# The second layer's first product in seven half-size products per pair of token tiles (Strassen) instead of eight

## The chip, the cores and the metric

The kernel runs on one core of one Trainium2 chip. The metric is the device time of one execution in microseconds, lower is better. Before the change three runs took 957.3, 959.89 and 960.03 us; their median, 959.89 us, is the time before.

## The reference

Three layers run one after the other, all in float32.

```
attn: state = gamma[h]*state + k_t v_t^T ;  y_t = scale * q_t state      (B,H,S,D = 4,8,768,64)
x  = y as (3072, 512)
ff1: x = elu(x @ w_in) @ w_out                                           (512 -> 2048 -> 512)
ff2: h = x @ w_in2                                                       (512 -> 1024)
     e = exp(h - max h);  solu = h * e / (sum e + 1e-9)
     ln = (solu - mean) / sqrt(var + 1e-6) * g_ln ;  out = ln @ w_out2   (1024 -> 512)
```

The weights arrive as float64; the kernel turns them into float32 itself.

## The kernel before

Every float32 operand of the two feed-forward layers is split into a high part of type fp32r and a low part, the rest. A product is then three matmuls (`mm3`, L63 to L67): high by high, high by low, low by high.

**FF1** works on six blocks (`tb`) of 512 tokens with 16 steps each, one step `s` per 128 hidden columns: `ff1_in(s)` (L255) is 12 matmuls into one of two PSUM banks `hp`, `elu_a` and `elu_b` (L265, L274) compute the activation on ScalarE and VectorE, GpSimd subtracts the high part to get `gl` (L290), and two steps later `ff1_out(s-2)` (L296) adds 12 matmuls into four banks `acc`. A bank `hp` is free for `ff1_in(s+2)` when `elu_b(s)` has read it. After a block, y goes to DRAM. Attention for later tokens runs between the steps of the first five blocks.

**FF2** works on 24 tiles of 128 tokens (L521 to L540). For tile `i`, `load_y` and `split_y` fetch and split y; `ff2_in(i)` (L333) makes h (128 tokens by 1024) in 24 matmuls; `norm_a` and `norm_b` (L342, L359) are max, exp, the product z, its mean and the sum of squares; `transpose(i-1)` (L367) transposes the z of the tile before in 8 matmuls, ScalarE and VectorE split it (`zh`, `zl`), and `ff2_out(i-2)` (L379) is 24 matmuls. The banks of h alternate between two places (`psr` and `ps2`).

**Weights.** `prep_w(order, n)` (L128) is a pipeline by slots: in slot `n`, ScalarE takes the absolute value of weight `n+1` and GpSimd clamps it (`clamp_w`, L98), VectorE builds the float32 bits of weight `n` in three instructions (`bits_w`, L104 to L108), the high part of weight `n-2` is a ScalarE copy and the low part a VectorE subtraction (L117, L125), and SyncE issues the load of weight `n+3`. The 16 weights of FF2 (`order2`: 8 of `w2i`, then 8 of `w2o`, which are first multiplied by `g_ln`, L114) are prepared during FF1's last block, one slot per step.

Nothing is reordered by a scheduler: each engine executes its instructions in the order in which the code writes them, and waits on semaphores between engines.

Of the kernel before, what the change touches and what calls it, by code (L numbers as in the profile page):

```python
# [43 lines left out]
def tile_retention_ffn(ctx, tc, k_t, qk_dup, qkv, w_in1, w_out1, w_in2, w_out2, g_ln, dmask, odec, kdec, ident_in, out):  # L44
# [5 lines left out]
    wa_p = ctx.enter_context(tc.tile_pool(name="wa", bufs=32))  # L50

# [17 lines left out]
    with tc.manual_schedule():  # L69
        ph1 = ExitStack()  # L70
        psh = ph1.enter_context(tc.tile_pool(name="psh", bufs=2, space=PSUM))
        ps = ph1.enter_context(tc.tile_pool(name="ps1", bufs=1, space=PSUM))
        pha = ExitStack()
# [3 lines left out]
        wb_p = ph1.enter_context(tc.tile_pool(name="wb", bufs=32))  # L77
        x_p = ph1.enter_context(tc.tile_pool(name="x", bufs=1))
# [10 lines left out]
        raw_t, abs_t, w1i, w1o, w2i, w2o = {}, {}, {}, {}, {}, {}  # L89
        srcs = {"w1i": w_in1, "w1o": w_out1, "w2i": w_in2, "w2o": w_out2}  # L90
        dsts = {"w1i": w1i, "w1o": w1o, "w2i": w2i, "w2o": w2o}
# [6 lines left out]
        def clamp_w(x):  # L98
            a = stage_p.tile([P, 512], U32, tag="wt", name="wt")
            nc.scalar.activation(a.bitcast(F32), raw_t[x][:, :, 1].bitcast(F32), AF.Abs)  # L100
            nc.gpsimd.tensor_scalar(a.bitcast(F32), a.bitcast(F32), E_MAX, E_MIN, ALU.min, ALU.max)
            abs_t[x] = a

        def bits_w(x):  # L104
            t, b = raw_t.pop(x), abs_t[x]
            nc.vector.tensor_scalar(b, b, 3, 0x3FFFFFF8, ALU.logical_shift_left, ALU.bitwise_and)
            nc.vector.scalar_tensor_tensor(b, t[:, :, 1], 0xC0000000, b, ALU.bitwise_and, ALU.bitwise_or)  # L107
            nc.vector.scalar_tensor_tensor(b, t[:, :, 0], 29, b, ALU.logical_shift_right, ALU.bitwise_or)  # L108

        def high_w(x):  # L110
            name, f = x
            w = abs_t[x].bitcast(F32)
            if name == "w2o":
                nc.vector.tensor_scalar(w, w, g_sb[:, f:f + 1], None, ALU.mult)  # L114
            pool, tag = (wb_p, "wb") if name == "w1o" else (wa_p, "wa")
            hi = pool.tile([P, 512], F32R, tag=tag, name=f"{name}h")
            nc.scalar.copy(hi, w)  # L117
            dsts[name][f] = hi

        def low_w(x):  # L120
            name, f = x
            w, hi = abs_t.pop(x).bitcast(F32), dsts[name][f]
            pool, tag = (wb_p, "wb") if name == "w1o" else (wa_p, "wa")
            lo = pool.tile([P, 512], F32R, tag=tag, name=f"{name}l")
            nc.vector.tensor_tensor(lo, w, hi.bitcast(F32), ALU.subtract)  # L125
            dsts[name][f] = (hi, lo)

        def prep_w(order, n):  # L128

            at = lambda i: order[i] if 0 <= i < len(order) else None  # L130
            if at(n - 2):
                high_w(at(n - 2))
# [4 lines left out]
            if at(n - 2):  # L137
                low_w(at(n - 2))
            if at(n + 3):
                load_w(at(n + 3))  # L140
# [4 lines left out]
        order2 = [("w2i", j) for j in range(2 * KD)] + [("w2o", j) for j in range(NF2)]  # L145
# [150 lines left out]
        def ff1_out(s):  # L296
# [8 lines left out]
            if f == NF1 - 1:  # L305
                for m in range(KD):
                    yt = yt_p.tile([P, TB], F32, tag="yt", name="yt", bufs=3) if m < 3 else e_p.tile([P, TB], F32, tag="e", name="yt")
# [12 lines left out]
        def load_y(i):  # L320
            t = yi_p.tile([P, KD, P], F32, tag="yin", name="yin")
            nc.sync.dma_start(out=t, in_=y_dr[i // CPB][i % CPB])
            yin[i] = t

        def split_y(i):
            t = yin.pop(i)
            yh = ys_p.tile([P, KD, P], F32R, tag="yh", name="yh")
            yl = ys_p.tile([P, KD, P], F32R, tag="yl", name="yl")
            nc.vector.tensor_copy(yh, t)
            nc.gpsimd.tensor_tensor(yl, t, yh.bitcast(F32), ALU.subtract)  # L330
            ysp[i] = (yh, yl)

        def ff2_in(i):  # L333
            yh, yl = ysp.pop(i)
            hp = (psr if i % 2 == 0 else ps2).tile([P, 2, 512], F32, tag="hp", name="hp2", bufs=1)
            for n in range(2):
                for cc in range(KD):
                    wh, wl = w2i[2 * cc + n]
                    mm3(hp[:, n, :], yh[:, cc, :], yl[:, cc, :], wh, wl, cc == 0, cc == KD - 1)
            h2[i] = hp  # L340

        def norm_a(i):  # L342
            hp = h2.pop(i)
            st = sm_p.tile([P, 8], F32, tag="st", name="st")
            if i == 0:
                e, z = xf[:, :2], xf[:, 2:]
# [32 lines left out]
        def ff2_out(i, kks=range(NF2)):  # L379
            zh, zl = zt_t[i]  # L380
# [56 lines left out]
        for s in range(NS + LAG):  # L437
            tb, k = divmod(s, NF1)
            n = PPB + LEAD + s
            u = n // 2  # L440
            if s < NS:
                ff1_in(s)
                elu_a(s, tb == 0)
                if k == NF1 - 1 and tb + 1 < NB:
                    split_xh(tb + 1, range(KD))
                    elu_b(s, tb == 0)
# [17 lines left out]
            if s < NS and (k < NF1 - 1 or tb + 1 == NB):  # L464
                elu_b(s, tb == 0)
            if s == NS + LAG - 1:
                ff2_in(0)
                split_y(2)
                norm_a(0)
                norm_b(0)  # L470
# [24 lines left out]
            if n == NPR - 1:  # L495
# [13 lines left out]
                prep_w(order2, -1)  # L509
            if tb == NB - 1:  # L510
                prep_w(order2, k)
                if k in (1, 2, 3):
                    load_y(k - 1)
                if k in (9, 11):
                    split_y((k - 9) // 2)
            if tb == NB:
                prep_w(order2, NF1 + k)
# [3 lines left out]
        for i in range(N2):  # L521
            if i + 3 < N2:
                load_y(i + 3)
            if i == 0:
                continue
            ff2_in(i)
            if i == 1:
                norm_a(i)
            if i + 2 < N2:
                split_y(i + 2)  # L530
            transpose(i - 1)
            if i > 1:
# [69 lines left out]
```

## Time and profile before

| | |
|---|---|
| runs, us | 957.3, 959.89, 960.03 (median 959.89) |
| the profiled execution | 957.76 us, of which the span of instructions is 955.9 us |
| TensorE busy | 928.9 us, 97% of the span, 4776 matmuls |
| VectorE, ScalarE, GpSimd busy | 494.7, 347.4 and 341.5 us |
| FF1's last block | about 573 to 663 us of the span |
| FF2 | from about 668 us to the end |

Matmuls are pipelined, so the recorded length of one overlaps the next; what one costs is the distance between two starts. A line of the timeline is one instruction, with its start, its length, engine, line, operands, and in brackets the idle time ahead of it. On VectorE and GpSimd a recorded length includes the time in which an instruction that was already issued waited inside the engine.

### The profile page before, as it was taken

The numbers are of one execution on the slowest core, as the hardware profiler recorded it, in microseconds if no ns is written. First come the engines' busy times: TensorE is split into PE (matmuls) and PEld (weight loads), VectorE is DVE, ScalarE is ACT, GpSimd is POOL, SyncE is SP. The second block draws the span as 40 slices with busy tenths as digits, with TensorE's granted clock in tenths as the row PEclk, the third lists the DMA queues.
The fourth block names the chain that finished last, engine by engine and source line by source line (L and its number), as shares of the span: only waits on it lengthen the run. The fifth ranks groups of instructions, "written<-read, shape, count | busy, mean of one in ns | idle before, by whom it ended". The sixth has DMA issues, their size and how long they took to land.

```text
span 955.9 us, 12630 instructions
## 1 busy us (share of the span) xinstructions
PE 928.9 (97%) x4776; PEld 760.0 (80%) x4776; DVE 494.7 (52%) x973; ACT 347.4 (36%) x629; POOL 341.5 (36%) x343
## 2 busy tenths in 40 slices
PE   6899999999999999999999999999999999999998
PEld 5677777888788887878788887888788888888886
DVE  3899997333443345333534328898633333333332
ACT  1355554333333334333332324443333333333332
POOL 2333232444534444444443423444322222222220
PEclk9999999999999999999999999999999999999999
DMA  8655551421142212322232214330211111111101
GB/s 253 195 177 179 182 171 39 121 78 53 64 121 78 77 48 78 113 78 77 70 91 77 80 67 138 95 91 20 77 45 45 45 45 44 45 45 45 45 23 44
DMA packets 43836, 82.67 MB, mean 86 GB/s; under 512 B 4096, under 2 KB 21120, under 8 KB 43776
## 3 DMA queue, kind: packets, MB, share of 16 engines
q1 hardware_dynamic: 43776, 81.88, 27.3%
q8 instruction: 37, 0.61, 0.3%
q14 instruction: 23, 0.19, 0.1%
HBM read 69.28 MB, written 12.58 MB: 86 GB/s over the span
## 4 chain that ended last, share of the span: by engine, by line
PE 79%; DVE 13%; DMA 2%; issue 2%; ACT 2%; SPq 1%; POOL 0%; ACTq 0%; DVEq 0%
PE hp L66 11%; PE hp L67 11%; PE hp L65 11%; PE acc L66 7%; PE acc L67 7%; PE acc L65 7%; PE op L66 5%; PE op L65 5%; PE op L67 5%; PE sc_bank L199 3%; PE yu_bank L219 2%; DVE wt L107 2%; PE tp L374 2%; DVE wt L108 2%; DVE xl L250 1%
## 5 line engine op out<-in xcount | busy, mean ns | idle before, releaser
L290 POOL TENSOR_TENSOR gl<-e,gh 128x512 fp32r<-128x512 f32 x80 | 108.1, 1351 | 249.2 <-ACT gh L282 201.7
L67 PE MATMUL acc<-gh,w1ol 128*128 128x512 f32 x384 | 150.7, 392 | 3.5 <-DVE w1ol L125 3.5
L67 PE MATMUL hp<-xh,w1il 128*128 128x512 f32 x384 | 150.4, 392 | 1.2 <-DVE w1il L125 1.2
L65 PE MATMUL acc<-gh,w1oh 128*128 128x512 f32 x384 | 151.2, 394 | 0.0
L66 PE MATMUL hp<-xl,w1ih 128*128 128x512 f32 x384 | 149.8, 390 | 1.1 <-DVE xl L250 0.9
L65 PE MATMUL hp<-xh,w1ih 128*128 128x512 f32 x384 | 149.9, 390 | 0.7 <-ACT xh L245 0.7
L66 PE MATMUL acc<-gl,w1oh 128*128 128x512 f32 x384 | 150.0, 391 | 0.0
L282 ACT CAST gh<-e 128x512 fp32r<-128x512 f32 x96 | 59.7, 622 | 199.7 <-DVE e L281 148.5
L271 ACT ACTIVATE e<-hp 128x512 f32<-128x512 f32 x80 | 47.8, 598 | 148.2 <-PE hp L67 147.3
L67 PEld LDWEIGHTS acc<-gh,w1ol 128*128 128x128 f32 x384 | 72.1, 188 | 21.2 <-DVE w1ol L125 6.3
L202 DVE TENSOR_TENSOR pt<-sa,sc_bank 128x256 f32<-128x256 f32 x60 | 25.3, 421 | 122.8 <-ACT sa L201 121.9
L67 PEld LDWEIGHTS hp<-xh,w1il 128*128 128x128 f32 x384 | 72.1, 188 | 18.9 <-DVE w1il L125 4.4
L66 PEld LDWEIGHTS hp<-xl,w1ih 128*128 128x128 f32 x384 | 72.1, 188 | 17.4 <-DVE xl L250 1.9
L65 PEld LDWEIGHTS hp<-xh,w1ih 128*128 128x128 f32 x384 | 72.1, 188 | 15.8 <-ACT xh L245 1.1
L65 PEld LDWEIGHTS acc<-gh,w1oh 128*128 128x128 f32 x384 | 72.2, 188 | 13.3 <-issue 0.5
L66 PEld LDWEIGHTS acc<-gl,w1oh 128*128 128x128 f32 x384 | 72.1, 188 | 12.8
L65 PE MATMUL op<-w2oh,zh 128*128 128x512 f32 x192 | 76.7, 399 | 0.0
L228 DVE TENSOR_TENSOR xf<-yu_bank,od_sb 128x256 f32<-128x256 f32 x43 | 18.1, 421 | 110.0 <-PE yu_bank L223 88.1
L66 PE MATMUL op<-w2ol,zh 128*128 128x512 f32 x192 | 74.8, 390 | 0.0
L67 PE MATMUL op<-w2oh,zl 128*128 128x512 f32 x192 | 74.8, 390 | 0.0
L67 PE MATMUL hp<-w2ih,yl 128*128 128x512 f32 x192 | 74.8, 389 | 0.0
L65 PE MATMUL hp<-w2ih,yh 128*128 128x512 f32 x192 | 74.8, 389 | 0.0
(101 smaller groups left out, 1573.1 us busy)
## 6 DMA issues: line engine op xcount, KB each, us to landing
in<-in_qkv SPq DMA_DIRECT2D x48, 384.0 KB, 4.4
qk<-in_qk_dup SPq DMA_DIRECT2D x30, 512.0 KB, 3.6
raw<-in_w_in SPq DMA_DIRECT2D x24, 512.0 KB, 4.3
raw<-in_w_out SPq DMA_DIRECT2D x24, 512.0 KB, 3.7
y_dr<-yt SPq DMA_DIRECT2D x24, 256.0 KB, 3.2
yin<-y_dr SPq DMA_DIRECT2D x24, 256.0 KB, 2.8
out<-ot SPq DMA_DIRECT2D x24, 256.0 KB, 2.0
kblk<-in_k_t SPq DMA_DIRECT2D x36, 64.0 KB, 4.5
```

The source lines that it names most:

```text
L65: nc.tensor.matmul(o, lh, rh, start=first, stop=False)
L66: nc.tensor.matmul(o, lh, rl, start=False, stop=False)
L67: nc.tensor.matmul(o, ll, rh, start=False, stop=last)
L107: nc.vector.scalar_tensor_tensor(b, t[:, :, 1], 0xC0000000, b, ALU.bitwise_and, ALU.bitwise_or)
L108: nc.vector.scalar_tensor_tensor(b, t[:, :, 0], 29, b, ALU.logical_shift_right, ALU.bitwise_or)
L199: nc.tensor.matmul(sc[:, j].rearrange("p a t -> p (a t)"), k2[:, 2 * i + j, :], q2[:, 2 * i + j].rearrange("p a t -> p (a t)"), start=True ...
L202: nc.vector.tensor_tensor(pt, sa, sc[:, :, 0, :], ALU.add)
L219: nc.tensor.matmul(yu[j * D:(j + 1) * D, i, 0, :], v[:, j * D:(j + 1) * D], pt[:, j, :], start=(c == 0), stop=True)
L271: nc.scalar.activation(e, h_t[s], AF.Exp)
L282: nc.scalar.copy(gh, e)
L290: engine.tensor_tensor(gl, e, gh.bitcast(F32), ALU.subtract)
L374: nc.tensor.transpose(tp[:, m, :], z[:, n, m * P:(m + 1) * P], ident)
```

## The change

FF2 now works on 12 pairs of tiles. In `h = y @ w_in2`, a pair's y (256 tokens by 512) and the weight (512 by 1024) are cut into two by two blocks, and the two by two blocks of h come from seven products in place of eight, with the sums of the Winograd form of Strassen's algorithm. Each product is 6 matmuls of 512 columns (two chunks of 128 rows times `mm3`), so a pair has 42 of them where two tiles had 48. Pair 0 has two more, which open the banks of c12 and c21.

- `combine` makes four sums of weight blocks (`t1` to `t4`) on VectorE; they are split like weights, in slots of `prep_w` that follow (`later`). `order2` becomes: four `w2i`, two `w2o`, four `w2i`, six `w2o`. Slot `n` stands in step `s = 79 + n` (before: 80 + n), FF1's last step is 95. `combine` runs in slots 5 and 11, the sums' parts are split in slots 6 to 9 and 12 to 15. The preparation starts one step earlier, each weight's load is issued one slot later (two raw buffers in place of four; weight 1 is loaded twice), and the clamped weights have three buffers in place of four.
- `split_y` makes four sums of y blocks on GpSimd, then splits seven blocks at once (128x1792). For pair 0 the sums stand in slot 5's step, the split in slot 7's; for pair 1 the sums in slot 13's, the split behind the block.
- `ff2_in(p)` has seven products with copies in PSUM by ScalarE and additions in PSUM by VectorE between them. The two tiles' banks `c0` and `c1` have one place each. The transposes of the tile two before (`between`) stand in the middle of it.
- Even pairs have their split operands in `ys_p`, odd ones in the place of FF1's x (`x_p`), so pair 0 is split during the last block. `ff2_in(0)` stands right after FF1's last `ff1_in`; `c1` is in the two `hp` banks.
- In the last block the activation uses two ScalarE instructions (relu, exp) and one on VectorE, as it did in the first block, and `gl` stays on GpSimd.

```diff
         def clamp_w(x):
-            a = stage_p.tile([P, 512], U32, tag="wt", name="wt")
+            a = stage_p.tile([P, 512], U32, tag="wt", name="wt", bufs=3 if x[0][1] == "2" else 4)
...
+        def combine(k):
+            b11, b12, b21, b22 = (xf[:, q] for q in range(4))
+            t1 = stage_p.tile([P, 512], F32, tag="t1", name="t1", bufs=1)
+            nc.vector.tensor_tensor(t1, b12, b11, ALU.subtract)
+            nc.vector.tensor_tensor(b12, b22, b12, ALU.subtract)
+            nc.vector.tensor_tensor(b22, b22, t1, ALU.subtract)
+            nc.vector.tensor_tensor(b21, b21, b22, ALU.subtract)
+            for name, w in (("t3", b12), ("t4", b21), ("t2", b22), ("t1", t1)):
+                later.append((name, k, w))
...
+            if later:
+                name, k, w = later.pop(0)
+                x = (name, k)
+                todo.append((x, w, high_w(x, w)))
...
-            if at(n + 3):
-                load_w(at(n + 3))
+            if at(n - 2) and at(n - 2)[0] == "w2i" and at(n - 2)[1] // 2 == 3:
+                combine(at(n - 2)[1] % 2)
+            if at(n + (3 if order is order1 else 2)):
+                load_w(at(n + (3 if order is order1 else 2)))
...
+        for k, js in enumerate((range(2), range(2, NF2))):
+            order2 += [("w2i", 2 * q + k) for q in range(4)] + [("w2o", j) for j in js]
...
+            if 0 in parts:
+                nc.gpsimd.tensor_tensor(s1, a21, a22, ALU.add)
+                nc.gpsimd.tensor_tensor(s2, s1, a11, ALU.subtract)
+                nc.gpsimd.tensor_tensor(s3, a11, a21, ALU.subtract)
+                nc.gpsimd.tensor_tensor(s4, a12, s2, ALU.subtract)
+            if 1 in parts:
+                nc.vector.tensor_copy(ysp[p][0], t[:, 1:])
+            if 2 in parts:
+                nc.gpsimd.tensor_tensor(yl, t[:, 1:], yh.bitcast(F32), ALU.subtract)
...
+            product(c11, 0, "b11", True)
+            nc.scalar.copy(c12, c11)
+            product(c22, 3, "t1", True)
+            nc.scalar.copy(p5, c22)
+            product(c11, 1, "b21", False)
+            product(c12, 4, "t2", False)
+            nc.scalar.copy(c21, c12)
+            nc.vector.tensor_tensor(c12, c12, p5, ALU.add)
+            if between is not None:
+                transpose(between, (0,))
+            product(c21, 5, "t3", False)
+            nc.vector.tensor_tensor(c22, c21, p5, ALU.add)
+            if between is not None:
+                transpose(between, (1,))
+            product(c12, 6, "b22", False)
+            product(c21, 2, "t4", False)
...
-            if s == NS + LAG - 1:
+            if s == NS:
+                phh.close()
+                psr1 = right.enter_context(tc.tile_pool(name="psr1", bufs=1, space=PSUM, side="right", reuse_waits="tile"))
+                split_y(1, (1, 2))
                 ff2_in(0)
...
-            if tb == NB:
-                prep_w(order2, NF1 + k)
+            if s >= NS - NF1 - 2:
+                prep_w(order2, s - (NS - NF1 - 1))
...
+        load_y(2)
+        norm_b(0)
+        norm_a(1)
+        norm_b(1)
+        split_y(2)
+        load_y(3)
+        for p in range(1, N2 // 2):
+            i = 2 * p
+            ff2_in(p, i - 2)
+            norm_a(i)
+            if i > 2:
+                ff2_out(i - 3)
+            norm_b(i)
+            norm_a(i + 1)
+            transpose(i - 1)
+            ff2_out(i - 2)
+            norm_b(i + 1)
+            if p + 2 < N2 // 2:
+                split_y(p + 2)
+            if p + 3 < N2 // 2:
+                load_y(p + 3)
```

VectorE in one step of the last block, a step whose slot has a `w2o` weight to split (L numbers are each file's own). Before:

```order
L280 TENSOR_SCALAR e<-e 128x512
L281 TENSOR_TENSOR e<-e,hp 128x512
L114 TENSOR_SCALAR wt<-wt,g_sb 128x512
L106 TENSOR_SCALAR wt<-wt 128x512
L107 SCALAR_TENSOR_TENSOR wt<-raw,wt 128x512
L108 SCALAR_TENSOR_TENSOR wt<-raw,wt 128x512
L125 TENSOR_TENSOR w2ol<-wt,w2oh 128x512
```

After the change, the step with slot 13:

```order
L319 SCALAR_TENSOR_TENSOR e<-e,hp 128x512
L153 TENSOR_SCALAR wt<-wt,g_sb 128x512
L109 TENSOR_SCALAR wt<-wt 128x512
L110 SCALAR_TENSOR_TENSOR wt<-raw,wt 128x512
L112 SCALAR_TENSOR_TENSOR wt<-raw,wt 128x512
L129 TENSOR_TENSOR w2ol<-wt,w2oh 128x512
L129 TENSOR_TENSOR t4l<-xf,t4h 128x512
```

The activation has one instruction less, and a sum's low part (`t4l`) has come behind the weight's.

ScalarE in the same step of the change:

```order
L323 CAST gh<-e 128x512
L123 CAST w2oh<-wt 128x512
L123 CAST t4h<-xf 128x512
L102 ACTIVATE wt<-raw 128x512
L309 ACTIVATE e<-hp 128x512
L310 ACTIVATE e<-e 128x512
```

The absolute value of the next weight (L102) stands ahead of the next step's relu and exp (L309, L310), as it stood ahead of the exp before.

ScalarE in FF2, two tiles of before:

```order
L375 CAST zh<-tp 128x512 x2
L351 ACTIVATE e_7140,st<-hp_7094,st 128x1024
L361 ACTIVATE e_7140,st<-z 128x1024
L389 ACTIVATE ot<-op,rs 128x512
L375 CAST zh<-tp 128x512 x2
L351 ACTIVATE e_7229,st<-hp_7183,st 128x1024
L361 ACTIVATE e_7229,st<-z 128x1024
L389 ACTIVATE ot<-op,rs 128x512
```

One pair of the change (`c` names the banks, `p` is p5):

```order
L414 COPY c_7194<-c_7194 128x512
L416 COPY p_7196<-c_7195 128x512
L419 COPY c_7195<-c_7194 128x512
L467 CAST zh<-tp 128x512 x2
L440 ACTIVATE e_7261,st<-c_7194,st 128x1024
L485 ACTIVATE ot<-op,rs 128x512
L450 ACTIVATE e_7261,st<-z 128x1024
L440 ACTIVATE e_7303,st<-c_7195,st 128x1024
L467 CAST zh<-tp 128x512 x2
L485 ACTIVATE ot<-op,rs 128x512
L450 ACTIVATE e_7303,st<-z 128x1024
```

The three copies are new. The last two rows, the output of tile `i-2` and the square of tile `i+1`, stand ahead of the next pair's first copy.

## Rows read from the trace of the kernel before

**Rows 1.** The page: busy time of the engines

```profile
PE 928.9 (97%) x4776; PEld 760.0 (80%) x4776; DVE 494.7 (52%) x973; ACT 347.4 (36%) x629; POOL 341.5 (36%) x343
```

**Rows 2.** Two stages: us, busy PE, PEld, DVE, ACT, POOL, PEclk, DMA share

```profile
640.00:660.00 20.00, 20.00 (x90) 16.53 (x90) 19.62 (x28) 8.96 (x16) 11.83 (x9) 1.00 0.15 50
800.00:900.00 100.00, 100.00 (x480) 83.59 (x479) 37.45 (x74) 34.54 (x61) 27.62 (x36) 1.00 0.15 48
```

**Rows 3.** Timeline of TensorE: ff2_in, transposes with ff2_out, the next tile

```profile
810.76 0.39 PE L65 MATMUL hp<-w2ih,yh 128*128 128x512 f32 x1
...
816.20 1.03 PE L374 MATMUL tp<-ident,z 128*128 128x128 f32 x8
...
822.53 0.39 PE L65 MATMUL hp<-w2ih,yh 128*128 128x512 f32 x1
```

**Rows 4.** Timeline of the other engines, the norm of one tile of FF2

```profile
806.89 1.22 DVE L350 TENSOR_REDUCE st<-hp 128x1 f32<-128x1024 f32 x1
...
808.14 1.12 ACT L351 ACTIVATE e<-hp,st 128x1024 f32<-128x1024 f32 x1 [2.00 <-DVE st L350]
...
809.83 1.28 DVE L354 SCALAR_TENSOR_TENSOR z<-hp,st,e 128x1024 f32<-128x1024 f32 x1
...
811.42 1.13 POOL L356 TENSOR_SCALAR z<-z,st 128x1024 f32<-128x1024 f32 x1 [5.11 <-DVE st L355]
...
812.58 1.06 ACT L361 ACTIVATE e<-z 128x1024 f32<-128x1024 f32 x1 [3.23 <-POOL z L356]
...
814.09 0.55 POOL L364 TENSOR_TENSOR rs<-st,half_n 128x1 f32<-128x1 f32 x1
```

**Rows 5.** Timeline of VectorE, one step of FF1's last block

```profile
650.52 0.41 DVE L280 TENSOR_SCALAR e<-e 128x512 f32<-128x512 f32 x1
650.97 0.69 DVE L281 TENSOR_TENSOR e<-e,hp 128x512 f32<-128x512 f32 x1
651.57 0.48 DVE L114 TENSOR_SCALAR wt<-wt,g_sb 128x512 f32<-128x512 f32 x1
651.97 0.42 DVE L106 TENSOR_SCALAR wt<-wt 128x512 uint32<-128x512 uint32 x1
652.43 0.69 DVE L107 SCALAR_TENSOR_TENSOR wt<-raw,wt 128x512 uint32<-128x512 uint32 x1
653.15 1.66 DVE L108 SCALAR_TENSOR_TENSOR wt<-raw,wt 128x512 uint32<-128x512 uint32 x1
654.74 1.09 DVE L125 TENSOR_TENSOR w2ol<-wt,w2oh 128x512 fp32r<-128x512 f32 x1
655.75 0.41 DVE L280 TENSOR_SCALAR e<-e 128x512 f32<-128x512 f32 x1
```

**Rows 6.** Groups by line: count, busy us and mean ns, idle before

```profile
L290 POOL TENSOR_TENSOR gl<-e,gh 128x512 fp32r<-128x512 f32 x80 | 108.1, 1351 | 249.2 <-ACT gh L282 201.7 <-issue 44.8 <-DVE wt L106 2.4
...
L101 POOL TENSOR_SCALAR wt<-wt 128x512 f32<-128x512 f32 x48 | 43.0, 896 | 84.2 <-DVE wt L108 61.8 <-ACT wt L100 22.4
...
L166 POOL TENSOR_TENSOR in<-in,kd_sb 128x256 f32<-128x256 f32 x48 | 32.9, 686 | 41.1 <-DMA in<-in_qkv 24.1 <-PE hp L67 9.0 <-DMA kd_sb<-in_kdec 4.1
L100 ACT ACTIVATE wt<-raw 128x512 f32<-128x512 f32 x48 | 32.2, 671 | 23.7 <-DMA raw<-in_w_in 21.4 <-DMA raw<-in_w_out 2.2
L330 POOL TENSOR_TENSOR yl<-yin,yh 128x512 fp32r<-128x512 f32 x24 | 31.1, 1297 | 50.0 <-PE hp L67 47.4 <-DVE yh L329 2.7
...
L269 ACT ACTIVATE e<-e 128x512 f32<-128x512 f32 x16 | 10.1, 632 | 0.5
...
L268 ACT ACTIVATE e<-hp 128x512 f32<-128x512 f32 x16 | 9.4, 585 | 2.9 <-PE hp L67 2.9
...
L312 ACT COPY yt<-acc 128x512 f32<-128x512 f32 x12 | 6.4, 584 | 0.0
```

**Rows 7.** Waits of TensorE: us in total, times, longest

```profile
PE tp L374 <- DVE zl L376: 1.5, 1, 1.5
```

**Rows 8.** DMA issues: KB each, median us to landing

```profile
raw<-in_w_out SPq DMA_DIRECT2D x24, 512.0 KB, 3.7
```

More of the change, by code (lines that the diff above doesn't have):

```diff
@@ L120, in low_w @@
[L120 to L124, printed above, removed]
-            nc.vector.tensor_tensor(lo, w, hi.bitcast(F32), ALU.subtract)
-            dsts[name][f] = (hi, lo)
+            if name == "w1o":
+                return wb0_p if f < NF1 // 2 else wb1_p, "wb"
+            return (wb0_p, "wb") if name[0] == "t" else (wa_p, "wa")
@@ L333, in ff2_in, with load_y @@
[L333 to L340, printed above, removed]
+        def load_y(p):
+            t = yi_p.tile([P, 8, 2, P], F32, tag="yin", name="yin")
+            src = lambda i: y_dr[i // CPB][i % CPB]
+            nc.sync.dma_start(out=t[:, 1:3].rearrange("p q k t -> p (q k) t"), in_=src(2 * p))
+            nc.sync.dma_start(out=t[:, 0], in_=src(2 * p + 1)[:, :2])
+            nc.sync.dma_start(out=t[:, 3], in_=src(2 * p + 1)[:, 2:])
+            yin[p] = t
@@ new lines, in y_home, with ff2_in, product @@
+        def y_home(p):
+            if p % 2 == 0:
+                return [ys_p.tile([P, 7, 2, P], F32R, tag=tag, name=tag) for tag in ("yh", "yl")]
+            return [x_p.tile([P, 8, 2, P], F32R, tag=tag, name=name)[:, 1:] for tag, name in (("xh", "yh"), ("xl", "yl"))]
+        def ff2_in(p, between=None):
+            yh, yl = ysp.pop(p)
+            c0 = psr.tile([P, 2, 512], F32, tag="c0", name="c0", bufs=1)
+            c1 = psr1.tile([P, 2, 512], F32, tag="c1", name="c1", bufs=1)
+            c11, c12, c21, c22 = c0[:, 0], c0[:, 1], c1[:, 0], c1[:, 1]
+            if p == 0:
+                for c in (c12, c21):
+                    nc.tensor.matmul(c, yh[:, 0, 0], w2c["b11", 0][0], start=True, stop=True)
+            def product(o, a, b, first):
+                for k in range(2):
+                    lh, ll, (rh, rl) = yh[:, a, k], yl[:, a, k], w2c[b, k]
+                    for n, (l, r) in enumerate(((lh, rh), (lh, rl), (ll, rh))):
+                        nc.tensor.matmul(o, l, r, start=first and k + n == 0, stop=k == 1 and n == 2, skip_group_check=True)
+            p5 = yt_p.tile([P, 512], F32, tag="yt", name="p5")
+            product(c11, 0, "b11", True)
[14 more added lines that the diff above has]
+            product(c21, 2, "t4", False)
+            h2[2 * p], h2[2 * p + 1] = c0, c1
```

160 lines of the change are left out of this document (85 added, 75 removed).

## The prediction

> **What bounds the kernel now.** The page first: TensorE is busy for 928.9 us of the 955.9 [rows 1]. Then the stages: in FF2 it has no idle time and every other engine has over half of its own free, while in FF1's last block VectorE is busy for 19.62 us of 20 beside a full TensorE [rows 2]. So FF2 is bound by the number of matmuls, and the last block by TensorE with VectorE just behind. Then the timeline of TensorE. `ff2_in` takes 816.20 - 810.76 = 5.44 us for 24 matmuls, 0.2267 us each, and the 8 transposes with `ff2_out` take 822.53 - 816.20 = 6.33 us, which leaves 0.89 us for the transposes [rows 3]. A step of FF1 has 24 matmuls too: 5.44 us.
>
> **What the change saves.** Per pair 6 matmuls go, 72 in all, and pair 0 adds two: 70 x 0.2267 = 15.9 us less. The one wait of TensorE at FF2's start, 1.5 us for `zl` [rows 7], goes with the order that made it; what is late there next is counted below. The transposes stay the same. A product takes 1.36 us, and a pair 9.52 us of products, 10.88 us of `ff2_out` and 1.78 us of transposes: 22.2 us against 23.5 for two tiles.
>
> **What the weights' preparation costs.** One step of VectorE in the last block [rows 5], from start to start: activation 0.45 + 0.60, `g_ln` 0.40, bits 0.46 + 0.72 + 1.59, low part 1.01, together 655.75 - 650.52 = 5.23 us. Two of these rows are stretched. L108 takes 1.66 us where L107, the same operation, takes 0.69, and L125 takes 1.09 where L281 takes 0.69. GpSimd's `gl` (1.35 us) and clamp (0.90 us) [rows 6] run then, so they hold VectorE up by 0.97 and 0.40 us, 0.4 to 0.5 less than they last. I price every GpSimd instruction beside VectorE by that: its length less 0.4.
>
> The Trainium skill, "SBUF — State Buffer", section "Who interferes with whom", says that a VectorE instruction with two SBUF inputs and a GpSimd instruction that reads SBUF share one read interface, and that whoever issues first keeps it for the whole instruction. By the whole length a step of before would be 0.9 us longer and not fit TensorE's 5.44 us; the trace has it at 5.23, so the row's share is what I use.
>
> A step after the change: activation 0.60, bits 1.79, one low part 0.60, held up 1.4: 4.4 us where the slot has one low part, 5.4 with a second one (a sum's) and `g_ln`. Against TensorE's 5.44 us VectorE's lag grows thus:
> - Slot 5: `combine`, 4 x 0.60 = 2.4 us, and pair 0's four sums on GpSimd, the nearest row the 128x256 multiplication L166 at 0.686 us [rows 6], so 0.3 us of hold each, 1.2 us. 8.0 us, lag 2.5.
> - Slot 6: 5.4 us, no change. Slot 7: also the copy of y's high part, 3.5 times the 0.41 us of L280 [rows 5], 1.4 us. Lag 3.9.
> - Slot 8: GpSimd's `yl` of 128x1792, 3.5 x 1.297 = 4.5 us [rows 6]; the activation covers 0.6 more, so it holds VectorE for 3.5 us. 8.5 us, lag 7.
> - Slots 9 and 10 need only 4.4 us, but with two raw buffers a load starts when the bits of two slots ago are done: 3.7 us of DMA [rows 8], then absolute value 0.67, relu 0.59 and exp 0.63 [rows 6], activation, bits. That is 10.2 us for two slots. Lag 6.3.
> - Slot 11: `combine` again, lag 7.6.
> - Slots 12 to 14: a `w2o` weight keeps its buffer until its low part is made, so with three buffers ScalarE's absolute value waits for that, and the next step's relu and exp stand behind it. A ring of 0.60 + 0.40 + 1.79 + 0.97 + 0.60 on VectorE, 0.67 + 0.59 + 0.63 on ScalarE and 0.15 for the hand-overs: 6.4 us per step, lag 10.5. Pair 1's four sums on GpSimd add 1.2. Slot 15 gives 0.4 back: lag 11.3.
>
> TensorE can wait for this at each `hp` bank (some 6 us of slack), but in the end all of it is due: pair 0 writes `c1`, the two `hp` banks, as soon as FF1's last `ff1_in` is done, and VectorE must have read the last one. Without lag it reads it 0.4 us before FF1's `ff1_out` of the step is over; the bank then waits for lag less some 0.8: **10.5 us**. The bounds: 0 if the lag stays under 0.8, and 14 if every GpSimd instruction holds VectorE for its whole length in the slots that have more than before.
>
> **What the pairs cost.** Times from U, the end of a pair's last product.
> - Pair 0 has no transposes inside: product 7 waits for ScalarE's copy in PSUM, 0.58 us [rows 6] and two hand-overs: 0.9 us.
> - Pair 1: `c1` has one place, so product 2 (into c22) waits for z of tile 1. By [rows 4] z ends 809.83 + 1.28 - 806.89 = 4.2 us after the max begins. For tile 0 the max starts at U - 1.1 and z ends at U + 3.1. Then VectorE has the last `w2o` weight and two copies of y, which wait for FF1's last products at U + 5.4. Max of tile 1 from 6.3, exp behind the square of tile 0, z done at 10.5. TensorE could start that product at U + 6.8: 3.7 us. Then ScalarE does the square of tile 1, 13.64 - 11.11 = 2.5 us after z's end [rows 4], before it makes the first copy, so product 3 waits until 13.8 where it could start at 11.9: 1.9 us. Together 5.6.
> - Pair 2: only one `ff2_out` lies between. By the same steps z of tile 3 ends at U + 9.0 against 7.7, and the copy at 12.1 against 10.4: 3.0.
> - Pairs 3 to 11: two `ff2_out` lie between (11.8 us with the transposes), z of the second tile ends at 10.6, well ahead of 13.1. On ScalarE the output of tile i-2 (from 12.0), the square (to 13.9) and the first copy end at 14.5, as product 2 does: 0.1. GpSimd's rs follows, ending 2.06 us after the square's start [rows 4], then four sums (2.8 us), then VectorE's 1.4 us copy, ahead of the addition that product 6 needs: it is ready 0.2 us late. I take 0.3 per pair, 2.7 in all, between 0 (nothing late) and 1.0 per pair (sums, or copies and additions in PSUM, half as long again as their nearest rows).
> - The end: the transposes of the last two tiles stand back to back on two banks, and the second waits for copy and subtraction (0.58 + 0.69 us) of the first: 1.4.
>
> The covers are thus GpSimd and ScalarE work that ends within 0.3 us of TensorE's need; if it runs late, the whole of it shows.
>
> **Sum.** -15.9 - 1.5 + 10.5 + 0.9 + 5.6 + 3.0 + 2.7 + 1.4 = +6.7 us. The profiled execution took 957.8 us, so it would take 964.5. The median of the runs is 2.1 higher, 959.9: I predict **966.6**.
>
> **Rivals.**
> 1. *The weights are ready in time.* VectorE's idle gaps and GpSimd's work interleave so that the lag at slot 15 stays under 0.8 us, and the 10.5 us go: 959.9 - 3.8 = 956, and 948 if pairs 1 and 2 also hide their waits. For it: an activation with one VectorE instruction in place of two frees 0.45 us a step, 7 us over the block. Against it: the block's added instructions need 2 x 2.4 + 8 x 0.60 + 1.4 us on VectorE alone, 11 us, and GpSimd's 4.5 us in one piece have no place beside it. Chance 0.25.
> 2. *Half the lag.* The ring over ScalarE does not close because the buffers come free earlier, and sums and `combine` overlap: a lag of 5, and 960.5. Chance 0.14.
> 3. *A slower chain in every pair.* It decides from 0.3 us per pair on: ScalarE and VectorE read and write PSUM in the new copies and additions, which no row of before shows, and four sums on GpSimd stand ahead of the copy of y. At 1.0 us per pair 6 us more: 973. Chance 0.14.
>
> That the change doesn't do what it says is no rival: the matmuls are fewer in the program itself, and each costs the same 512 columns.
> The forecast has 0.47.
>
> **How the numbers follow.** A run of this kernel can be told from no change beyond about 0.3%, 2.9 us: 957.0 to 962.8. Faster is rival 1 without its upper edge, 0.23. The same is rival 2 and that edge, 0.16. Slower is the forecast with rival 3, 0.61. The forecast's own range, by the bounds of the preparation (8 to 14) and of the pairs (0 to 0.6), is 961 to 973. The range for 8 in 10 reaches into rivals 1 and 3: 951 to 975.
>
> **What would show it.** In the profile after: 4706 matmuls or so; a pair of FF2 in the middle 22.2 to 22.8 us; TensorE idle for some 10 us between slot 8 and the first product of pair 0, ended by VectorE's activation; L112, L110 and the sums on VectorE stretched while `yl` runs; waits of TensorE on z (L443) and on the copy L414 for pairs 1 and 2 alone. I am wrong if TensorE runs through the last block without idle time, or if every pair waits for more than half a microsecond.

## The result and the profile after

Four runs of the changed kernel took 967.0 to 969.86 us, median **968.54**; four of the kernel before 957.3 to 961.61, median 959.96. The ratio is 1.0091, 95% interval 1.0062 to 1.0121: 0.9% slower, clear of the noise and as forecast (966.6 us; slower had a chance of 0.61). The profiled execution took 969.56 us, 11.8 more than that of before.

The page's busy time of the engines, which answers to [rows 1]:

```profile
PE 924.1 (95%) x4706; PEld 751.8 (78%) x4706; DVE 516.0 (53%) x983; ACT 377.1 (39%) x687; POOL 392.0 (41%) x379
```

The 70 matmuls are gone. Two stages, with the columns of [rows 2] (the same stretches of time), and between them the stretch around pair 0's start:

```profile
640.00:660.00 20.00, 19.59 (x87) 15.90 (x86) 17.87 (x25) 10.84 (x19) 8.90 (x7) 1.00 0.37 123
672.00:674.00 2.00, 0.00 (x0) 0.00 (x0) 1.97 (x3) 1.97 (x5) 1.27 (x1) 1.00 0.00 0
674.00:676.00 2.00, 0.00 (x0) 0.00 (x0) 1.97 (x4) 0.54 (x1) 0.00 (x0) 0.72 0.00 0
676.00:678.00 2.00, 1.18 (x3) 0.99 (x4) 1.19 (x4) 1.14 (x2) 0.51 (x1) 0.50 0.00 0
...
800.00:900.00 100.00, 100.00 (x477) 83.30 (x476) 48.02 (x88) 41.63 (x76) 45.59 (x48) 1.00 0.15 50
```

FF2 is bound by TensorE as before, with all others below half. In the last block TensorE now has gaps, and from 672 to 676 us it does nothing while VectorE is busy throughout. The waits of TensorE from the last block's second step on, in place of the one of [rows 7] (us in total, times, longest):

```profile
PE c L404 <- DVE e L319: 5.8, 1, 5.8
...
PE c L410 <- DVE z L443: 4.4, 2, 3.7
...
PE c L410 <- ACT c L414: 3.0, 2, 1.5
PE hp L67 <- DVE e L319: 1.5, 3, 0.6
...
PE acc L68 <- POOL gl L331: 1.5, 2, 0.9
PE tp L466 <- DVE zl L471: 1.2, 1, 1.2
...
PE c L410 <- ACT c L419: 0.7, 1, 0.7
```

18.1 us of waits, each at a place that the prediction names but `acc`, which waits for GpSimd's `gl`: for the weights' preparation (L404, `hp`, `acc`: 8.8), pairs 1 and 2 (z, L414), pair 0's third copy (L419), the end (L466). What it does not name is in TensorE's timeline at pair 0, in the start times:

```profile
670.68 0.39 PE L404 MATMUL c<-w2ih,yh 128*128 128x512 f32 x1
676.82 0.79 PE L404 MATMUL c<-w2ih,yh 128*128 128x512 f32 x1 [5.75 <-DVE e L319]
677.41 0.63 PE L410 MATMUL c<-w2ih,yh 128*128 128x512 f32 x1
677.84 0.63 PE L410 MATMUL c<-w2il,yh 128*128 128x512 f32 x1
...
743.20 0.39 PE L410 MATMUL c<-w2ih,yh 128*128 128x512 f32 x1
...
765.51 0.39 PE L410 MATMUL c<-w2ih,yh 128*128 128x512 f32 x1
```

Behind the wait two matmuls start 0.43 us apart where they should 0.2267: the granted clock is 0.50 there (the windows above), the level of 1.2 GHz. That holds for 11 matmuls. A pair in the middle takes 765.51 - 743.20 = 22.31 us.

The profiled executions also differ by 3.8 us ahead of the last block, in code of which the change alters only buffers (the block's first matmul starts at 578.25, before at 574.47). There the change's execution has the clock at 0.50 in two short stretches and that of before in none:

```profile
34.00:36.00 2.00, 2.00 (x17) 1.54 (x14) 1.08 (x4) 0.83 (x2) 1.09 (x1) 0.50 0.33 114
...
266.00:268.00 2.00, 2.00 (x6) 1.55 (x5) 1.66 (x4) 0.24 (x1) 0.00 (x0) 0.50 0.96 369
```

Three traces of the experiments below that have the change's code up to there (fill_both, pair0_later, late_weights) have no window below 1.00 ahead of the last block, and it begins at 572.9 to 574.4 us in them. So the 3.8 us are of this execution and not of the code's work there, and below, beside each time, stands **the stretch from the last block's first matmul to the start of the last matmul of all**, read from one trace each, which leaves that out: 951.81 - 574.47 = 377.34 us before, 963.39 - 578.25 = 385.14 after, 7.8 more.

### The profile page after: what moved, and what is told of

Read it like the earlier page. It is cut to its first block, busy times and chain, and to the rows that moved or that the text cites. A ratio compares the mean times of both kernels' runs of the same rounds, so it can differ in the third digit from the quotient of the medians.

```text
span 967.7 us, 12672 instructions
## 1 busy us (share of the span) xinstructions
PE 924.1 (95%) x4706; PEld 751.8 (78%) x4706; DVE 516.0 (53%) x983; ACT 377.1 (39%) x687; POOL 392.0 (41%) x379
## 4 chain that ended last, share of the span: by engine, by line
PE 71%; DVE 19%; issue 4%; ACT 3%; DMA 3%; POOL 1%; SPq 0%; DVEq 0%; ACTq 0%; POOLq 0%
PE c L410 11%; PE hp L68 6%; PE hp L69 6%; PE hp L67 6%; PE acc L67 6%; PE acc L68 6%; PE acc L69 6%; PE op L69 4%; PE op L68 4%; PE op L67 4%; DVE wt L110 3%; PE sc_bank L240 3%; PE yu_bank L260 2%; DVE wt L109 2%; PE tp L466 2%
## 5 line engine op out<-in xcount | busy, mean ns | idle before, releaser
L312 ACT ACTIVATE e<-hp 128x512 f32<-128x512 f32 x64 | 38.2, 597 | 122.6 <-PE hp L69 122.6
L103 POOL TENSOR_SCALAR wt<-wt 128x512 f32<-128x512 f32 x48 | 41.0, 855 | 98.1 <-DVE wt L112 61.8
L269 DVE TENSOR_TENSOR xf<-yu_bank,od_sb 128x256 f32<-128x256 f32 x43 | 18.1, 421 | 113.3 <-PE yu_bank L264 91.4
L385 POOL TENSOR_TENSOR yl<-yin,yh 128x1792 fp32r<-128x1792 f32 x12 | 48.8, 4066 | 16.7 <-DVE yh L382 16.7
```

The lines of the kernel that those rows point to most:

```text
L312: nc.scalar.activation(e, h_t[s], AF.Exp)
L385: nc.gpsimd.tensor_tensor(yl, t[:, 1:], yh.bitcast(F32), ALU.subtract)
```

## The experiments

### Four places for the clamped weights (four_places)

```diff
-a = stage_p.tile([P, 512], U32, tag="wt", name="wt", bufs=3 if x[0][1] == "2" else 4)
+a = stage_p.tile([P, 512], U32, tag="wt", name="wt", bufs=4)
```

> The changed kernel with four buffers for the clamped weights in place of three, nothing else. In the trace of the change VectorE's activations (L319) in slots 12 to 14 stand 6.34, 6.35 and 7.51 us apart, and ScalarE waits 2.1 to 3.2 us there for the low part of the w2o weight before its absolute value (L102), with relu and exp behind it. Theory (the ring over ScalarE closes because of the third buffer): these steps go back to 5.4 to 5.5 us (6.6 where pair 1's sums stand), the wait ahead of pair 0 falls from 5.75 to about 2.5 us, 2 to 3.5, and the waits of TensorE inside the block in slots 12 to 14 (together 2 us) to under 1: some 4 us less, 964 to 965. Rival (VectorE, held up by GpSimd, sets the pace there by itself): the steps stay above 6 us and the time within 1 us of the change. If the shorter idle time also leaves TensorE's granted clock at its upper level, 2 us more.

Measured: 966.25 us, ratio to before 1.0071 (1.0045 to 1.0096); the stretch 384.55, 0.6 less. VectorE's activations that begin slots 12 to 14 and the one behind, first in the change:

```profile
650.80 0.68 DVE L319 SCALAR_TENSOR_TENSOR e<-e,hp 128x512 f32<-128x512 f32 x1
...
657.14 0.69 DVE L319 SCALAR_TENSOR_TENSOR e<-e,hp 128x512 f32<-128x512 f32 x1 [1.29 <-ACT e L310]
...
663.49 0.69 DVE L319 SCALAR_TENSOR_TENSOR e<-e,hp 128x512 f32<-128x512 f32 x1 [1.30 <-ACT e L310]
...
671.00 0.69 DVE L319 SCALAR_TENSOR_TENSOR e<-e,hp 128x512 f32<-128x512 f32 x1 [1.29 <-ACT e L310]
```

and with four places:

```profile
647.89 0.68 DVE L319 SCALAR_TENSOR_TENSOR e<-e,hp 128x512 f32<-128x512 f32 x1
...
653.27 0.68 DVE L319 SCALAR_TENSOR_TENSOR e<-e,hp 128x512 f32<-128x512 f32 x1
...
659.20 0.67 DVE L319 SCALAR_TENSOR_TENSOR e<-e,hp 128x512 f32<-128x512 f32 x1
...
665.54 0.67 DVE L319 SCALAR_TENSOR_TENSOR e<-e,hp 128x512 f32<-128x512 f32 x1
```

The ring is real: with three places VectorE waits 1.3 us in each of these steps for ScalarE's exp, which stands behind the absolute value, and a step takes 6.34, 6.35 and 7.51 us. With four no wait is left and they take 5.38, 5.93 and 6.34. But two of the three are still over TensorE's 5.44, so the expectation holds in part, and the rival too: VectorE alone, held up by GpSimd, is too slow there without any wait. The preparation's waits fall from 8.8 to 6.3 us, where some 4 us less were expected. The stretch gains so little of that since the clock, which fell once in the change, falls twice here (behind pair 0's wait of 4.8 us and behind pair 1's of 3.7).

### Pair 0's split in earlier steps (early_split)

```diff
-if k in (1, 9):
+if k in (0, 9):
     load_y(k // 8)
-if k in (4, 12):
+if k in (2, 12):
     split_y(k // 8, (0,))
-if k == 6:
+if k == 3:
     split_y(0, (1, 2))
```

> The changed kernel with pair 0's y loaded in the last block's first step in place of its second, its four sums on GpSimd in the third step in place of the fifth, and its split (copy and yl) in the fourth in place of the seventh. In the trace of the change VectorE still waits 2.1, 2.3 and 0.5 us for ScalarE in the first five steps and has no such gap in slots 5 to 8. Theory (what GpSimd's sums and yl hold up on VectorE is lag only where VectorE has no gap to take it): the gaps take 2 to 3 us of the 4.5 us of yl and copy, and the waits of TensorE in the block and ahead of pair 0, together 10.3 us in the change, fall by 2 to 3 us. Rival (the lag at slot 15 is set by the ring of slots 12 to 15 alone, whatever came before): no gain, within 0.5 us; or the loads of the weights, which then stand behind y's in the DMA queues, come later and cost 1 to 2 us.

Measured: 966.56 us, 1.0076 (1.0053 to 1.01); the stretch 384.72. The waits inside the block fall from 3.0 to 1.9 us, the one ahead of pair 0 is 5.8 as before. Both theories hold in part: the early lag is taken up by gaps and by TensorE's own waits. But in both traces TensorE waits at an `hp` bank once more, for the activation that begins slot 14 (0.59 us in the change, 0.60 here), and is level with VectorE there, whatever came before. The wait ahead of pair 0 comes from what follows, slots 14 and 15, whose steps are the change's to 0.01 us: VectorE needs 7.52 + 5.08 = 12.6 us for them, and TensorE has 25 matmuls, 5.7 us, and 0.6 us of another wait until it asks for `c1`.

### yl of pair 0 on VectorE (yl_on_vector)

```diff
-nc.gpsimd.tensor_tensor(yl, t[:, 1:], yh.bitcast(F32), ALU.subtract)
+(nc.vector if p == 0 else nc.gpsimd).tensor_tensor(yl, t[:, 1:], yh.bitcast(F32), ALU.subtract)
```

> The changed kernel with pair 0's yl (128x1792) made by VectorE itself in place of GpSimd. In the trace of the change the GpSimd instruction takes 4.07 us and VectorE's L109 beside it 3.98 us in place of 0.42, so it is held for 3.56 us. Theory (GpSimd's instruction holds VectorE for its length less some 0.5 us, and the lag of slot 8 is that): VectorE's own yl takes 3.5 x 0.60 = 2.1 us, the other instruction its 0.42, so slot 8 is 1.4 us shorter, and the waits of TensorE right behind it (1.09 us for gl, 0.70 us for the activation) nearly go; the wait ahead of pair 0 stays at 5.7 to 5.8 us, as it did with the early split: 1.5 to 2 us less. Rival (L109 was late for another reason, such as its own input): L109 stays long, and slot 8 gets 2 us longer.

Measured: 967.09 us, 1.0089 (1.0063 to 1.0114); the stretch 384.78. The timeline of VectorE and GpSimd in the change:

```profile
626.27 0.67 DVE L319 SCALAR_TENSOR_TENSOR e<-e,hp 128x512 f32<-128x512 f32 x1
...
626.50 4.07 POOL L385 TENSOR_TENSOR yl<-yin,yh 128x1792 fp32r<-128x1792 f32 x1 [2.90 <-DVE yh L382]
...
626.87 3.98 DVE L109 TENSOR_SCALAR wt<-wt 128x512 uint32<-128x512 uint32 x1
...
634.67 0.68 DVE L319 SCALAR_TENSOR_TENSOR e<-e,hp 128x512 f32<-128x512 f32 x1
```

and with yl on VectorE:

```profile
625.04 2.02 DVE L385 TENSOR_TENSOR yl<-yin,yh 128x1792 fp32r<-128x1792 f32 x1
626.99 0.68 DVE L319 SCALAR_TENSOR_TENSOR e<-e,hp 128x512 f32<-128x512 f32 x1
627.58 0.42 DVE L109 TENSOR_SCALAR wt<-wt 128x512 uint32<-128x512 uint32 x1
```

L109 is back at 0.42 us, so it was GpSimd's yl that held it, for 3.56 us: 0.37 of yl's 4.07 us had passed when L109 began, and L109 ended 0.28 us behind yl. The prediction had 3.5, from a longer yl (4.5) and larger deductions (0.6 and 0.4). VectorE does the same work in 2.02 us. The waits inside the block fall from 3.0 to 2.0, the one ahead of pair 0 stays at 5.8. That is the expected kind and somewhat less of it, and the clock again falls behind pair 1's wait too, so the stretch gains 0.4 where 1.5 to 2 us were expected.

### Matmuls in the wait (fill, fill_both)

```diff
-for c in (c12, c21):
+for c in (c12,) * 25 + (c21,):
     nc.tensor.matmul(c, yh[:, 0, 0], w2c["b11", 0][0], start=True, stop=True)
```

> The changed kernel with 24 more opening matmuls into c12 ahead of the one into c21, so that TensorE has 24 x 0.2267 = 5.4 us of matmuls in the 5.75 us in which it waits for the last activation. They add nothing that pair 0 keeps, since its first copy overwrites c12. In the trace of the change the granted clock falls from 1.00 to 0.50 in that wait, and 11 matmuls behind it start 0.43 us apart in place of 0.2267. Theory (TensorE without work is what lets the clock down): 1.00 through pair 0, its first product at the same time as before, pair 0 shorter by 11 x 0.2 = 2.2 us, time 966 to 966.5. Rival (the clock falls there for another reason, such as the work before): 0.50 as in the change and no gain, or, if the added matmuls end late, up to 1 us lost.

Measured: 966.28 us, 1.0064 (1.0034 to 1.0094); the stretch 384.80. The windows behind pair 0's wait and behind pair 1's:

```profile
676.00:678.00 2.00, 1.61 (x8) 1.01 (x7) 1.19 (x3) 1.14 (x2) 0.48 (x1) 1.00 0.00 0
...
700.00:702.00 2.00, 1.34 (x3) 0.60 (x3) 0.00 (x0) 1.95 (x4) 0.89 (x3) 0.50 0.00 0
702.00:704.00 2.00, 2.00 (x6) 1.53 (x5) 0.00 (x0) 0.00 (x0) 1.92 (x3) 0.50 0.02 4
```

Pair 0 runs at full clock, so TensorE's idle time was what let it down; but now the clock falls behind pair 1's wait of 3.73 us, behind which it had stayed up in the change, and the gain is gone: the stretch has 0.3 us less in place of 2.2. That the time is the expected one is luck. Hence both waits filled:

```diff
 product(c11, 0, "b11", True)
+if p == 1:
+    for _ in range(14):
+        nc.tensor.matmul(c12, yh[:, 0, 0], w2c["b11", 0][0], start=True, stop=True)
```

> The version fill (24 added matmuls in the wait ahead of pair 0) with 14 more (3.2 us) into c12 in pair 1, between its first and its second product, where TensorE waits 3.73 us for z; the copy that follows overwrites c12. In fill the clock stayed at 1.00 through pair 0, but fell to 0.50 behind the wait in pair 1, where 13 matmuls then started 0.43 us apart: from the last block's first matmul to the last matmul of all 384.80 us, the change 385.14, the kernel before 377.34. Theory (each of the two waits alone lets the clock down if the other did not, and the lowered clock is what the prediction's sum lacked): 1.00 through pairs 0 and 1 and 2 to 2.5 us less in that stretch, 382.3 to 382.8. Rival (the clock falls at the next wait of 1.5 us, for the copy): 0.50 behind it and no gain, 384.5 to 385.

Measured: 963.91 us, 1.0063 (1.0043 to 1.0083); the stretch 955.79 - 572.95 = 382.84, 2.3 less than the change, and no window below 1.00 from the last block to the last matmul. The lowered clock is worth 2.3 us of the 7.8.

### The square behind the next copies (late_square)

```diff
 nc.scalar.copy(p5, c22)
+if square is not None:
+    norm_b(square)
...
-norm_b(i + 1)
...
-ff2_in(p, i - 2)
+ff2_in(p, i - 2, i - 1)
```

> The changed kernel with the square and the scale of a pair's second tile (norm_b) moved behind the first two copies of the next pair, so that on ScalarE the copies stand ahead of the square, and on GpSimd the next sums ahead of the scale. Theory: the waits of TensorE for the first copy in pairs 1 and 2, 1.5 us each, go (3.0 to 3.4 us with what the matmul behind a wait costs), those for z (3.7 and 0.7) stay; time 965 to 965.5. Rival (something else is late at the same point: the copies come no earlier because ScalarE waits for another thing, or the third copy, now behind the square, is late in every pair): the waits move to the third copy, 1 us or more in pairs 1 and 2 or some tenths in every pair, and the time stays or rises.

Measured: 964.88 us, 1.0055 (1.0034 to 1.0076); the stretch 383.85. The two waits for L414 are gone from the list and none took their place: 3.0 us, as expected. The stretch gains 1.3, since the clock fell in pair 1 too.

### Pair 0 one ff1_out later (pair0_later)

```diff
-    ff2_in(0)
-    norm_a(0)
 if s >= LAG:
     ff1_out(s - LAG)
+if s == NS:
+    ff2_in(0)
+    norm_a(0)
```

> The changed kernel with pair 0's products behind the next-to-last ff1_out in place of ahead of it. Theory (what TensorE waits for is VectorE, and the place of the 2.72 us of work only moves the wait): the wait ahead of pair 0 goes from 5.75 us to some 3 us ahead of ff1_out's gl and up to 0.5 ahead of c1, and pair 1, with one ff1_out in place of two between it and pair 0, waits 2.7 us longer for z (6.4 in place of 3.7): the time is that of the change within 1 us, but for the granted clock. Rival (the early place of pair 0 is what costs): 2.5 us or more less.

Measured: 963.72 us, 1.0061 (1.0034 to 1.0087); the stretch 383.62, 1.5 less. TensorE's waits:

```profile
PE c L410 <- DVE z L443: 6.5, 2, 5.8
...
PE acc L68 <- POOL gl L331: 2.3, 3, 0.9
...
PE acc L67 <- ACT gh L323: 1.6, 1, 1.6
```

The wait ahead of pair 0 splits into 1.6 and 0.85 us ahead of `ff1_out`, and pair 1 waits 5.82 us for z in place of 3.73. The place of the work moves the wait: of the 3.3 us that it gives, 2.1 come back one pair later. The stretch lies between the theory (within 1 us) and the rival (2.5 us or more). That the time is 4.8 us under the change's is mostly the first blocks: six of the seven runs had a mean granted clock of 0.995 or 0.996, the change's 0.991 to 0.993.

### The last weights behind the block (late_weights)

```diff
-if s >= NS - NF1 - 2:
-    prep_w(order2, s - (NS - NF1 - 1))
+if NS - NF1 - 2 <= s < NS - 1:
+    prep_w(order2, s - (NS - NF1 - 1), s < NS - 3)
...
+prep_w(order2, 14)
 split_y(1, (1, 2))
 ff2_in(0)
...
 norm_b(1)
+for n in (15, 16, 17):
+    prep_w(order2, n)
```

> The changed kernel with the weights of slots 14 to 17 taken out of the last block's last steps: slot 14 stands behind the last activation, ahead of pair 1's split, and slots 15 to 17 behind the norm of tile 1. The sums' parts (t2, t1) stay where they were. Theory (the wait ahead of pair 0 is VectorE's lag from the ring of the last slots, and the lag goes as soon as two steps carry no weight): with the last three activations of the trace of the change (663.49, 671.00, 676.09), the second comes at some 667 and the third at some 669, before TensorE asks for c1 at 670.7. So the wait of 5.75 us goes to under 0.5, the clock behind it stays up (2.2 us), and the waits in slots 8 to 13 (some 3 us) stay: 6 to 8.5 us less, 960 to 962.5, the lower gain if the clock then falls in pair 1's wait for z, as it did with the added matmuls. Rival (the lag is carried from the sums and yl of slots 5 to 8, and the last slots only show it): at least 3 us of the wait stay. Rival two: the moved weights delay pair 0's additions and the norm, and pairs 0 and 1 wait 3 us longer than in the change.

The new third argument of `prep_w`, where it is false, leaves the weights out and keeps the sums' parts.

Measured: 968.04 us, 1.0093 (1.0066 to 1.012); the stretch 385.67, no gain. TensorE's waits, and ScalarE ahead of pair 1's first copy:

```profile
PE c L410 <- ACT c L414: 10.5, 3, 7.2
...
PE c L410 <- DVE z L443: 4.4, 2, 3.7
```

```profile
690.46 1.06 ACT L450 ACTIVATE e<-z 128x1024 f32<-128x1024 f32 x1 [3.58 <-POOL z L445]
...
691.52 0.60 ACT L123 CAST w2oh<-wt 128x512 fp32r<-128x512 f32 x1
693.74 0.62 ACT L123 CAST w2oh<-wt 128x512 fp32r<-128x512 f32 x1 [1.62 <-DVE wt L153]
696.42 0.62 ACT L123 CAST w2oh<-wt 128x512 fp32r<-128x512 f32 x1 [2.06 <-DVE wt L153]
696.94 0.58 ACT L414 COPY c<-c 128x512 f32<-128x512 f32 x1
```

The theory on the block holds: the wait ahead of pair 0 is gone, so the last steps make it. Rival two holds as well: on ScalarE the copy that TensorE needs stands behind three high parts, each of which waits for VectorE, and 5.7 us of new wait in pair 1 (1.8 in pair 0), with the clock at 0.50 behind it, take it all back.

### All together (best, best2)

best joins the edits above but `fill` and `pair0_later` (yl of pairs 0 and 1 on VectorE), and changes the norm of the first two tiles and the end (parts of the edit):

```diff
+elif i == 1:
+    e = z = dm_sb.rearrange("p (n h) t -> p n (h t)", n=2)
...
 ff2_in(0)
-norm_a(0)
+norm_e(0)
+norm_e(1)
+norm_z(0)
+norm_z(1)
...
+transpose(N2 - 2)
 ff2_out(N2 - 3)
-transpose(N2 - 2)
 transpose(N2 - 1)
```

> All together: four places for the clamped weights, the early split, yl of pairs 0 and 1 on VectorE, the weights of slots 14 to 17 behind the block, the norm of tile 1 in the place of the attention's mask and interleaved with that of tile 0 right behind pair 0 (so that z of tile 1 is done before pair 1 asks for c22), the square behind the next pair's copies, and at the end the transposes of tile 22 ahead of ff2_out of tile 21. By the theory of the ledger, from the change's 968.5 us: the waits in the block 4.3 to 1, the wait ahead of pair 0 (6.3 us with its first matmul) to 0, the lower clock in FF2 2.4 to 0, pair 1 5.7 to 0.3, pair 2 2.7 to 0.8, the end 1.4 to 0: 20.9 us less, 947.6 us, 944 to 952, 1.2% under the kernel before. Rival (the waits only move: each step taken off uncovers the next engine's lateness): half of it or less, 958 and above.

Measured: 952.93 us, 0.9942 (0.9923 to 0.9961); the stretch 369.30. No wait in the block or ahead of pair 0, none for z in pair 1, none at the end. One is left that matters, that of late_weights; with it the time is 0.9 us above the expected range:

```profile
PE c L410 <- ACT c L414: 4.2, 1, 4.2
```

best2 spreads slots 15 to 17 (parts of the edit; `norm_e` and `norm_z` are the halves of `norm_a`). Slot 17 stands behind pair 1's first two copies, with the split of pair 2's y, and in pair 1 both tiles' `norm_e` stand ahead of their `norm_z`:

```diff
 nc.vector.tensor_tensor(c12, c12, p5, ALU.add)
+if slots[1]:
+    prep_w(order2, slots[1])
...
+load_y(2)
-ff2_in(0)
+ff2_in(0, slots=(None, 15))
 norm_e(0)
 norm_e(1)
+split_y(2, (0,))
...
-for n in (15, 16, 17):
-    prep_w(order2, n)
-split_y(2)
+prep_w(order2, 16)
...
-ff2_in(p, i - 2, i - 1)
+ff2_in(p, i - 2, i - 1, (17 if p == 1 else None, None))
```

> The version before (best), in whose trace TensorE still waits 4.25 us in pair 1 for the first copy: ScalarE makes it behind the high parts of three w2o weights (slots 15 to 17), each of which waits for VectorE. Here slot 15 stands in pair 0, behind the addition into c12, slot 16 behind the norm of tiles 0 and 1, slot 17 behind the first two copies of pair 1; pair 2's y is loaded and summed during pair 0; and in pair 1 the two maxima and exps stand ahead of the two z. Theory: the wait of 4.4 us, the lower clock behind it (1.5 us) and the wait of pair 2 for z (0.9 us) go, and only pair 0's wait for the third copy (0.9 us) is left: 6 to 7 us less than best's 952.9, 946 to 947. Rival (slot 15 in pair 0 delays the norm, or the split of pair 2 on GpSimd the additions): the wait comes back at z or at an addition, 2 to 4 us, 949 to 951.

Measured: **946.97 us, 0.9866 (0.9839 to 0.9893)**, faster than the kernel before by 1.3%; the stretch 363.91, 13.4 less than before. TensorE's waits from the last block's second step on:

```profile
PE c L410 <- DVE c L431: 1.1, 1, 1.1
...
PE c L410 <- ACT c L424: 0.7, 1, 0.7
```

and the two stages of [rows 2]:

```profile
640.00:660.00 20.00, 20.00 (x90) 16.58 (x89) 18.66 (x24) 10.63 (x19) 11.46 (x10) 1.00 0.37 129
800.00:900.00 100.00, 100.00 (x477) 83.31 (x476) 48.04 (x88) 42.80 (x77) 44.33 (x47) 1.00 0.13 43
```

TensorE is full in both, and of the 15.9 us of the matmuls and the 1.6 us of the old wait 13.4 come out at last.

## Why the prediction was right

The direction, the time and nearly every term held. Measured by distances of matmul starts (each start later than 0.2267 us behind the last one), so that a wait counts with the slower first matmul behind it:

| term | predicted, us | measured, us |
|---|---|---|
| 70 matmuls | -15.9 | -15.9 |
| old wait for zl | -1.5 | -1.6 |
| preparation: inside the block, ahead of pair 0 | +10.5 in one | +4.3, +5.9 |
| clock behind that wait | not named | +2.4 |
| pair 0, third copy | +0.9 | +1.0 |
| pair 1 | +5.6 | +5.7 |
| pair 2 | +3.0 | +2.7 |
| pairs 3 to 11 (measured: all eleven pairs that have transposes inside) | +2.7 | +1.3 |
| end | +1.4 | +1.5 |
| sum | +6.7 | +7.3 |

The stretch has +7.8; the rest are distances too small for the list.

**The preparation.** The ledger by slots is confirmed as a whole and mostly in its reasons. Slots 5 to 15 last 676.09 - 605.01 = 71.1 us in the trace; the prediction's 11 x 5.44 + 11.3 is the same. Slot 8 took 8.40 (8.5 predicted), slots 12 and 13 6.34 and 6.35 (6.4), slot 14 with pair 1's sums 7.51 (6.4 + 1.2). Two single slots were off, and cancel: slot 5 took 8.98 for 8.0, since GpSimd's sums took 1.07 to 1.19 us beside `combine` in place of the 0.69 of the row, and slots 9 and 10 took 8.96 for 10.2, which is also more than the rows named for it add up to (8.0, or 9.0 with `gl`'s hold of 0.97). That the lag would come due only at pair 0 was wrong in form: TensorE waited for 4.3 us of it inside the block, at `hp` and at `gl`, and 5.9 at the end. Rival 1 (ready in time) and rival 2 (the ring does not close) are excluded; four_places shows that without the ring more than half would have stayed (6.3 of 8.8 us of waits), as rival 2 had it.

The price of GpSimd's hold on VectorE, a length less 0.4, served the sum, but it was not read rightly. The prediction took the mean lengths of [rows 6], 1.35 and 0.90 us, for one step [rows 5]; in that step GpSimd's two instructions are longer, since they wait themselves:

```profile
652.45 1.81 POOL L290 TENSOR_TENSOR gl<-e,gh 128x512 fp32r<-128x512 f32 x1 [2.99 <-issue]
654.24 1.05 POOL L101 TENSOR_SCALAR wt<-wt 128x512 f32<-128x512 f32 x1
```

L108 ends at 654.81; without the hold it needs 0.69, so it was held until 654.12, which is 0.14 us ahead of the end of `gl` (654.26). L125 was held in the same way until 0.15 us ahead of the clamp's end, and L109 of the change until 0.14 ahead of the end of `yl`. So VectorE goes on when GpSimd's instruction is nearly over, and what it loses depends on when its own instruction began. The Trainium skill, "SBUF — State Buffer", section "Who interferes with whom", has the whole instruction, and the rows agree to 0.15 us. That the whole length would make a step of before 0.9 us too long came from the means. The section also says that a VectorE instruction with at most one SBUF input, outside the 2-port perf modes, does not contend with GpSimd, and the trace agrees for one whose other operands are in PSUM: in best an addition in PSUM took 0.70 us (start 693.68) while yl ran (692.56 to 696.61). L109 has one SBUF input too and was held; which mode it ran in no row says.

**The pairs.** z and the first copy came late in pairs 1 and 2 alone, by the amounts that the chain of durations gave. In pairs 3 to 11 nothing waits; what they lose is another thing, 0.1 us more for each of the first two matmuls behind the transposes in the middle of a pair (2.2 us in eleven pairs, less 0.9 that the same cost ahead of ten `ff2_out` of before). So rival 3 is excluded.

**The step that failed** is "What bounds the kernel now", which took 0.2267 us as the price of every matmul. Behind an idle TensorE the clock was at 1.2 GHz and a matmul cost 0.43 us, for 6 to 14 of them each time: 2.4 us here, and fill_both gives 2.3 for the whole stretch. The sum was made against an execution without it. That it still came within 1.1 us of the stretch is in part luck: the pairs from 3 on cost 1.4 us less than was taken for them, which hides more than half of the clock's 2.4. That the clock had also fallen by 3.8 us' worth in the first blocks of the profiled execution is not the code's work there (fill has the same code and the same two stretches, fill_both has the same code and neither), and the same happens to the kernel before: of its runs beside the experiments those with a mean granted clock of 1.000 took 955.6 to 958.4 us, those with 0.995 or less 960.8 to 964.1. The four runs of the change had 0.991 to 0.993. Why its runs have that more often than those of before stays open; it was not tried.

## What to carry to other kernels

A saving on a full engine counts only where all the others keep pace: write down, slot by slot, what the changed stage asks of each engine with the durations of the trace, holds included, and compare that with the step of the engine that you unload. Work that another engine must finish by one moment (weights for a later stage, a norm that frees a bank) goes off the stage that has no slack to one that has, but on every queue behind what is needed sooner. Take the waits off together: one at a time they gave 0.3 to 1.5 us of stretch or nothing, all of them 21.2.

## What the runs showed that was not expected

The clock does not follow a wait by its length alone. Behind pair 0's wait of 4.8 to 5.8 us it fell to 0.50 in all five traces that have that wait. Behind pair 1's wait of 3.73 us it stayed at 1.00 in the change and in late_weights, and fell in four_places, fill, early_split, late_square and yl_on_vector. In the first blocks it fell behind shorter waits, in some executions of the same code and not in others. Behind this wait, first in fill and then in fill_both, it fell to 0.50 (266 to 268 us) in the one and stayed at 1.00 in the other:

```profile
264.68 0.44 PE L260 MATMUL yu_bank<-pt,in 128*64 128x128 f32 x4 [1.85 <-DVE pt L244]
```

```profile
260.97 0.44 PE L260 MATMUL yu_bank<-pt,in 128*64 128x128 f32 x4 [1.85 <-DVE pt L244]
```

What decides it stays open. The Trainium skill, "TensorE: Matmul & The Clock Gate", section "Part 1: The HAM clock gate", says that an idle TensorE is put to half its clock; where it fell the traces agree, with 0.43 us per matmul in place of 0.2267. fill_both shows that matmuls into a place that is written anew kept the clock up through both of its filled waits.
